# Twelve attention units taken in six pairs: one score run and one softmax for two units

## The chip, the cores and the metric

The kernel runs on one core of a Trainium2 chip. The metric is the device time of one execution in microseconds (us); the time before is the median of three runs, 905.88 us (905.54 to 908.12). One further execution was recorded by the hardware profiler.

## The reference

Attention within chunks of 64 positions, then two dense stages on the 2304 x 512 result, all in float32:

```python
q_c, k_c, v_c = (t.reshape(4, 8, 9, 64, 64) for t in (q, k, v))
s = (q_c @ k_c.transpose(0, 1, 2, 4, 3)) / 8
e = exp(s - s.max(-1)); p = e / (e.sum(-1) + 1e-9)
x = (p @ v_c) as 2304 tokens x 512
x = ((x @ w_a) * (x @ w_b)) @ w_out                      # 512 -> 1536 -> 512
h = x @ w_in                                              # 512 -> 2048
g = (a0 + a1 h + a2 h2 + a3 h3) / (1 + |b0||h| + |b1|h2 + 1e-6)   # h2 = h*h, h3 = h*h*h
out = g @ moe2_w_out                                      # 2048 -> 512
```

## The kernel before

Dense products run as three matmuls each (high by high, high by low, low by high part of the operands, function mm3, whose lines are L252, L253 and L254). They keep TensorE occupied from the first third of the tokens on. The tokens go in three groups of 768. The first group's products with w_a and w_b are plain: 24 entries, each with two products of 128 x 384 outputs (ab_half), and each product is 12 matmuls. The other two groups' products follow in a second part (s_step), which wants the attention output x of these groups in several combinations (x_first, x_second make them on ScalarE and VectorE).

Attention is cut into 18 units of 128 tokens, two chunks of 64 by eight heads. A unit goes through these pieces: T, four PE transposes of k and four of q (a_transpose, L330) and a copy of each out of PSUM on ScalarE (L332); S, 32 score matmuls of 64 x 64 (a_scores, L347), then the maximum and the subtraction on VectorE (L353, L355); X, the exponential on ScalarE (a_exp, L361); E, sum, reciprocal and scaling on VectorE (a_soft, L366 to L369); P, four transposes of the probabilities (a_ptrans, L377) and a copy (L379); V, 32 matmuls of 64 x 64 with v (a_pv, L394) and two copies of the result (L404). Units 0 to 5 make the first token group, units 6 to 11 the second and 12 to 17 the third.

The pieces of the last twelve units are placed between the matmuls of the 24 entries by a list of due times. Every six dense matmuls (half of a product) the function half() first converts a quarter of a weight tile (w_until; L217, L219, L226, L194 on ScalarE, L199, L224, L234 on VectorE), then moves a clock by 0.5 and issues all pieces that are due, in order of due time and then of their entry in the list. Such a half step is called a step here; the times in the list are in units of two steps:

```python
FROM, PER, GAP = 6.0, 2.65, 2.0
times = (0, 0.5, 2, 3, 3.5, 5, 6.5)        # k, q, S, X, E, P, V
a_unit(2 * UH + n, FROM + PER * n + (GAP if n >= 2 * UH else 0), times)
```

PSUM has eight banks: four of pool ps_acc (dense products), one each with the tags a and b (ps_ab, scores and results of V), and two of pool ps_at (transposes), taken in turn. An instruction that writes a bank waits until the reader of what was in it is done. Each engine works through its own instructions in order. The loads of k and q have one buffer each: the load for the next unit is issued (queue SP, in order) behind the transposes that read the present one. Loads of v have two. The loads of raw weight tiles are on the same queue and wait there for the conversion that frees their buffer.

When the third unit of a half group is through V, x_first or x_second puts its passes over x in the list; x_second has fourteen, nine of them on VectorE, due over four time units.

Of the kernel before, what the change touches and what calls it, by code (L numbers as in the profile page):

```python
# [9 lines left out]
F32 = mybir.dt.float32  # L10
# [4 lines left out]
AF = mybir.ActivationFunctionType  # L15
ALU = mybir.AluOpType
AX = mybir.AxisListType
# [3 lines left out]
def chunk_attention_two_mlps(  # L21
# [34 lines left out]
    nc = tc.nc  # L56
    P = 128
    B, H, S, D = q.shape
# [3 lines left out]
    CH = 64  # L62
    NCH = S // CH
    HP = H // 2
    KD = DM // P
# [3 lines left out]
    SCALE = 1.0 / math.sqrt(D)  # L69
# [4 lines left out]
    GH = GT // 2  # L74
    UH = GH // P
    NQ = NT // GT
# [29 lines left out]
    ps_ab = ctx.enter_context(tc.tile_pool(name="ps_ab", bufs=1, space=PSUM))  # L106
    ps_at = ctx.enter_context(tc.tile_pool(name="ps_at", bufs=2, space=PSUM))
# [7 lines left out]
    ident = const.tile([P, P], F32, name="ident")  # L115
# [9 lines left out]
    p_X = s_X.enter_context(tc.tile_pool(name="X", bufs=1))  # L125
    s_x32 = ExitStack()
    p_x32 = s_x32.enter_context(tc.tile_pool(name="x32", bufs=2, side="right"))
# [4 lines left out]
    p_e = const  # L132
# [127 lines left out]
    todo = []  # L260
# [6 lines left out]
    n_todo = [0]  # L267
# [12 lines left out]
    raw = {}  # L280
    un = {}
# [12 lines left out]
    def a_tmp(u, name):  # L294
        if u >= UH:
            return p_t.tile([P, HP, P], F32, name=name, tag="T")
        n = n_t0[0] % 6
        n_t0[0] += 1
        return t_0[n // 3][:, n % 3]

    def a_load(u, *names):

        (b0, c0), (b1, c1) = divmod(2 * u, NCH), divmod(2 * u + 1, NCH)
        for nm, src in (("k", k), ("q", q), ("v", v)):
            if nm not in names or u >= NU:
                continue
            if u < 2 * UH:
                if ("raw", u) not in un:
                    un["raw", u] = p_X.tile([P, 3, H, D], F32, name="kqv", tag=f"X{NQ - 1}_{u + 1}")
                t = un["raw", u][:, "kqv".index(nm)]  # L310
            else:
                t = p_qk.tile([P, H, D], F32, name=nm, tag=nm, bufs=2 if nm == "v" else 1)
            if b0 == b1:
                parts = [(t, src[b0, :, c0 * CH:(c0 + 2) * CH, :])]
            else:
                parts = [
                    (t[c * CH:(c + 1) * CH], src[bb, :, cc * CH:(cc + 1) * CH, :])
                    for c, (bb, cc) in enumerate(((b0, c0), (b1, c1)))
                ]
            for dst, s in parts:  # L320
                nc.sync.dma_start(out=dst, in_=s.rearrange("h s d -> s h d"))
            raw[nm, u] = t

    def a_transpose(u, nm):

        t = raw.pop((nm, u)).rearrange("p (a b) d -> p a (b d)", b=2)
        pool, tag = (ps_acc, "acc") if u < UH else (ps_at, "at")
        ps = pool.tile([P, HP, P], F32, name="at", tag=tag)
        for hp in range(HP):
            nc.tensor.transpose(ps[:, hp, :], t[:, hp, :], ident)  # L330
        o = a_tmp(u, nm + "T")
        nc.scalar.copy(o, ps)  # L332
        un[nm + "T", u] = o

    def a_scores(u):

        qT, kT = un.pop(("qT", u)), un.pop(("kT", u))
        ps = [ps_ab.tile([P, HP, CH], F32, name="at", tag=tag) for tag in "ab"]  # L340
        for a in range(2):
            for c in range(2):
                for t in range(2):
                    for b in range(2):
                        r, half, cols = (slice(n * CH, (n + 1) * CH) for n in (b, t, c))
                        hp = 2 * a + t
                        nc.tensor.matmul(  # L347
                            ps[b][half, 2 * a + c, :], qT[r, hp, cols], kT[r, hp, cols], start=True, stop=True
                        )
        m = p_e.tile([P, 2, HP], F32, name="m", tag="m")  # L350
        e = a_tmp(u, "e").rearrange("p x (y d) -> p (x y) d", d=CH).rearrange("p (b x) d -> p b x d", b=2)
        for b in range(2):
            nc.vector.tensor_reduce(m[:, b], ps[b], AX.X, ALU.max)  # L353
        for b in range(2):
            nc.vector.tensor_tensor(  # L355
                e[:, b], ps[b], m[:, b].unsqueeze(2).to_broadcast([P, HP, CH]), ALU.subtract
            )
        un["e", u] = e.rearrange("p b x d -> p (b x) d")

    def a_exp(u):  # L360
        nc.scalar.activation(un["e", u], un["e", u], AF.Exp, scale=SCALE)  # L361
# [20 lines left out]
    def a_pv(u):  # L382

        pT, vv = un.pop(("pT", u)), raw.pop(("v", u))
        ps = []
        for c in range(2):
            pool, tag = (ps_acc, "acc") if u < UH else (ps_ab, "ab"[c])
            ps.append(pool.tile([P, HP, CH], F32, name="at", tag=tag))
        for hp in range(HP):
            a, t = divmod(hp, 2)  # L390
            for c in range(2):
                for h2 in range(2):
                    r, cols, half = (slice(n * CH, (n + 1) * CH) for n in (c, h2, t))
                    nc.tensor.matmul(  # L394
                        ps[c][cols, hp, :], vv[r, 2 * hp + h2, :], pT[r, 2 * h2 + a, half], start=True, stop=True
                    )
        g, at = divmod(u, 2 * UH)
        if g:
            if at % UH == 0:
                un["x32", g, at // UH] = p_x32.tile([P, KD, GH], F32, name="x32", tag="x32")  # L400
            t = un["x32", g, at // UH]
            for c in range(2):
                to = at % UH * P + c * CH
                nc.scalar.copy(t[:, :, to:to + CH], ps[c])  # L404
            if at % UH == UH - 1:
                (x_first if at < UH else x_second)(g)
            return
        out = [[t[:, :, u * P + c * CH:u * P + (c + 1) * CH] for t in (x_hi, x_lo)] for c in range(2)]
        for c, (hi, lo) in enumerate(out):
            nc.scalar.copy(hi, ps[c])  # L410

        def low():
            for c, (hi, lo) in enumerate(out):
                nc.vector.tensor_tensor(lo, ps[c], hi.bitcast(F32), ALU.subtract)

        un["lo", u] = low

    def x_hl(g, c, x):
        t = x_block(g, c)
        hi, lo = t[:, 0], t[:, 1]  # L420
        return (
            lambda: nc.scalar.copy(hi, x),
            lambda: nc.vector.tensor_tensor(lo, x, hi.bitcast(F32), ALU.subtract),
        )
# [32 lines left out]
    def a_unit(u, at, times):  # L457


        def piece(dt, *fs):  # L460
            for f in fs:
                todo.append((at + dt, n_todo[0], f))
                n_todo[0] += 1

        k, q, s, x, e, p, v = times
        if ("kT", u) not in un:
            piece(k, lambda: a_transpose(u, "k"), lambda: u >= 2 * UH and a_load(u + 1, "k"))
            piece(q, lambda: a_transpose(u, "q"), lambda: u >= 2 * UH and a_load(u + 1, "q"))
        piece(s, lambda: a_scores(u))
        piece(x, lambda: a_exp(u))  # L470
        piece(e, lambda: a_soft(u))
        piece(p, lambda: a_ptrans(u))
        piece(v, lambda: a_pv(u), lambda: u >= 2 * UH and a_load(u + 2, "v"))
        if u < 2 * UH:
            piece(v + 0.5, lambda: un.pop(("lo", u))())


    ca_t = const.tile([P, 4], F32, name="ca_t")
# [219 lines left out]
    y = {}  # L698
# [14 lines left out]
    h2 = {}  # L713
# [111 lines left out]
    for item in FIRST:  # L825
# [9 lines left out]
        what, u = item[:-1], int(item[-1])  # L835
# [12 lines left out]
    seq = [(i, h) for h in range(2) for i in range(4)] + [(i, h) for i in range(4, F1) for h in range(2)]  # L848
    for n in range(UH):
        a_unit(UH + n, 1.0 + 0.5 * n, (0, 0.5, 1.5, 2, 2.5, 3.5, 4.5))  # L850
    FROM, PER, GAP = 6.0, 2.65, 2.0
    times = (0, 0.5, 2, 3, 3.5, 5, 6.5)
    for n in range((NQ - 1) * 2 * UH):
        a_unit(2 * UH + n, FROM + PER * n + (GAP if n >= 2 * UH else 0), times)
    p_j2 = None
    preps = {}

# [12 lines left out]
        if op == 11 and t + 2 < F1:  # L870
            s_load(t + 2)

    END = math.ceil(2 * (FROM + PER * ((NQ - 1) * 2 * UH - 1) + GAP + times[-1] + 0.25)) / 2
    todo.append((END, n_todo[0], s_begin))
    n_todo[0] += 1
    for op in range(12):
        at = min(END + 2 + 0.5 * (op // 3), 2.0 * len(seq) - 0.5)
        todo.append((at, n_todo[0], lambda op=op: s_do(0, op)))
# [29 lines left out]
    for t in range(1, F1):  # L908

        if t == 1:  # L910
            at = [(0, m // 2) for m in range(12)]
        elif t == 2:
            at = [(2, m) for m in (3, 3, 4, 5)] + [(3, m) for m in (0, 1, 2, 3, 3, 4, 5, 6)]
        else:
            at = [(2 * t - 2 + m // 6, FILLS[m % 6]) for m in range(12)]
# [19 lines left out]
    for n, (i, g) in enumerate(seq2):  # L935
        place[:] = [n, 0]
        if n == len(seq2) - 1:
# [3 lines left out]
            t = p_x32.tile([P, 2, SIZES[0]], F32, name="g_raw", tag="x32")  # L941
# [98 lines left out]
```

## Time and profile before

| what | value |
|---|---|
| median of three runs | 905.88 us |
| the profiled execution's own time | 904.24 us |
| its span, first to last instruction | 902.5 us |
| granted TensorE clock over the span | 1.00 |
| busy share of PE, DVE, ACT over the span | 98%, 80%, 68% |
| stretch that holds the last twelve units | about 54 to 172 us |

PE is TensorE, PEld its weight loads, DVE is VectorE, ACT is ScalarE, POOL is GpSimd; SP issues loads. Matmuls overlap one another, so the time that a matmul takes from PE is read from the distance between starts, not from its duration.

### The profile page before, as it was taken

To read this page: it belongs to the slowest core of one execution; us is meant where nothing else is said; L and a number is where in the kernel's file an instruction comes from. 1 tells how busy PE (TensorE), PEld (TensorE's weight loads), DVE (VectorE), ACT (ScalarE), POOL (GpSimd) and SP (SyncE) were. 2 spreads that over 40 slices of the span, in tenths; PEclk is the share of its full clock that TensorE was granted. 3 is DMA by queue.
4 is the path that set the end of the run, shared out by engine and by line. 5 is a ranking of instruction groups with operands and counts; after the bars stand their busy time and mean duration, and the time that the engine had idled before them with its cause. 6 is when DMAs were issued, how large, how long until landed. Compare 5 with 4: busy or idle time off the path is not lost.

```text
span 902.5 us, 14772 instructions
## 1 busy us (share of the span) xinstructions
PE 883.7 (98%) x5532; PEld 788.0 (87%) x5532; DVE 723.3 (80%) x1321; ACT 612.7 (68%) x1105; POOL 63.9 (7%) x122
## 2 busy tenths in 40 slices
PE   6989999999999999999999999999999999999998
PEld 5879989999999999988888998888888888888987
DVE  5657788497878886578778599998889988988886
ACT  5857888445554553678777688877677667776775
POOL 0111111111111111100000000000000000000000
PEclk9999999999999999999999999999999999999999
DMA  9969886333343423778777200200020002000100
GB/s 233 263 200 263 251 239 171 106 130 126 127 146 123 147 85 105 245 250 277 261 243 256 94 1 1 82 1 1 1 93 1 1 1 82 0 1 1 48 1 36
DMA packets 107336, 105.83 MB, mean 117 GB/s; under 512 B 61440, under 2 KB 84480, under 8 KB 107264
## 3 DMA queue, kind: packets, MB, share of 16 engines
q1 hardware_dynamic: 99264, 79.71, 29.6%
q0 software_dynamic: 8000, 25.17, 7.5%
q8 instruction: 43, 0.70, 0.3%
q14 instruction: 29, 0.24, 0.1%
HBM read 74.98 MB, written 29.88 MB: 116 GB/s over the span
## 4 chain that ended last, share of the span: by engine, by line
PE 92%; DVE 4%; ACT 2%; DMA 1%; issue 0%; SPq 0%; DVEq 0%; ACTq 0%
PE h L254 7%; PE acc L254 7%; PE acc L253 7%; PE h L252 7%; PE h L253 7%; PE acc L252 7%; PE acc L682 5%; PE acc L683 5%; PE acc L685 5%; PE ab L252 3%; PE ab L254 3%; PE ab L253 3%; PE y L253 3%; PE y L254 3%; PE y L252 3%; PE q L252 2%
## 5 line engine op out<-in xcount | busy, mean ns | idle before, releaser
L254 PE MATMUL h<-y,w_i 128*128 128x512 f32 (+1 forms) x320 | 117.8, 368 | 0.0
L252 PE MATMUL h<-y,w_i 128*128 128x512 f32 (+1 forms) x320 | 117.8, 368 | 0.0
L253 PE MATMUL h<-y,w_i 128*128 128x512 f32 (+1 forms) x320 | 117.7, 368 | 0.0
L739 ACT ACTIVATE a_ring<-h 128x512 f32<-128x512 f32 (+1 forms) x80 | 44.1, 551 | 88.0 <-PE h L254 88.0
L580 ACT COPY s<-y 128x384 f32<-128x384 f32 x72 | 34.4, 480 | 80.0 <-PE y L254 79.9
L682 PE MATMUL acc<-g_hi,w_o 128*128 128x512 f32 (+1 forms) x240 | 86.9, 369 | 0.0
L683 PE MATMUL acc<-g_hi,w_o 128*128 128x512 f32 (+1 forms) x240 | 86.8, 368 | 0.0
L742 DVE SCALAR_TENSOR_TENSOR u<-u,cb_t,a_ring 128x512 f32<-128x512 f32 (+1 forms) x80 | 55.7, 696 | 30.2 <-ACT u L740 29.4
L254 PE MATMUL acc<-w_o,g_lo 128*128 128x512 f32 x191 | 74.7, 391 | 0.0
L253 PE MATMUL acc<-w_o,g_hi 128*128 128x512 f32 x191 | 74.6, 391 | 0.0
L252 PE MATMUL acc<-w_o,g_hi 128*128 128x512 f32 x191 | 74.3, 389 | 0.0
L253 PEld LDWEIGHTS h<-y,w_i 128*128 128x128 f32 x320 | 60.1, 188 | 8.8
L252 PEld LDWEIGHTS h<-y,w_i 128*128 128x128 f32 x320 | 60.1, 188 | 8.8
L254 PEld LDWEIGHTS h<-y,w_i 128*128 128x128 f32 x320 | 60.1, 188 | 7.4
L662 DVE TENSOR_TENSOR g_lo<-g_raw,g_hi 128x512 fp32r<-128x512 f32 (+1 forms) x60 | 38.2, 638 | 28.1 <-ACT g_hi L660 15.4
L685 PE MATMUL acc<-g_lo,w_o 128*128 128x512 f32 (+1 forms) x240 | 59.3, 368 | 0.0
L741 ACT ACTIVATE t<-h,ca_t 128x512 f32<-128x512 f32 (+1 forms) x80 | 59.0, 737 | 0.0
L752 DVE SCALAR_TENSOR_TENSOR u<-u,r 128x512 f32<-128x512 f32 (+1 forms) x80 | 50.6, 632 | 9.5 <-ACT r L751 9.5
L744 DVE SCALAR_TENSOR_TENSOR t<-t,ca_t,h 128x512 f32<-128x512 f32 (+1 forms) x80 | 55.6, 695 | 2.8
L751 ACT ACTIVATE r<-r,nlsh 128x512 f32<-128x512 f32 (+1 forms) x80 | 54.5, 682 | 2.6
L750 ACT ACTIVATE r<-u,nlsh 128x512 f32<-128x512 f32 (+1 forms) x80 | 55.6, 695 | 0.3
L753 DVE SCALAR_TENSOR_TENSOR t<-t,ca_t,r 128x512 f32<-128x512 f32 (+1 forms) x80 | 55.4, 692 | 0.0
(195 smaller groups left out, 2400.9 us busy)
## 6 DMA issues: line engine op xcount, KB each, us to landing
w_raw<-in_moe_w_out_dram SPq DMA_DIRECT2D x28, 512.0 KB, 3.9
g_d<-g POOLq DMA_DIRECT2D x72, 192.0 KB, 2.5
g_raw<-g_d SPq DMA_DIRECT2D x48, 256.0 KB, 4.2
w_raw<-in_moe_w_in_dram SPq DMA_DIRECT2D x16, 512.0 KB, 4.6
w_raw<-in_moe_w_a_dram SPq DMA_DIRECT2D x12, 512.0 KB, 4.8
w_raw<-in_moe_w_b_dram SPq DMA_DIRECT2D x12, 512.0 KB, 5.2
out_dram<-o SPq DMA_DIRECT2D x18, 256.0 KB, 2.4
y_d<-ys POOLq DMA_DIRECT2D x16, 256.0 KB, 4.1
```

Of the source, the lines that this page charges most:

```text
L252: nc.tensor.matmul(ps, wh, xh, start=first, stop=False, **kw)
L253: nc.tensor.matmul(ps, wh, xl, start=False, stop=False, **kw)
L254: nc.tensor.matmul(ps, wl, xh, start=False, stop=last, **kw)
L682: nc.tensor.matmul(acc[j][d], wh, gh, start=i == 0, stop=False)
L683: nc.tensor.matmul(acc[j][d], wl, gh, start=False, stop=False)
L685: nc.tensor.matmul(acc[j][d], cols(w, d)[0], gl, start=False, stop=i == F1 - 1)
L741: nc.scalar.activation(t, ps, AF.Identity, scale=ca_t[:, 3:4], bias=ca_t[:, 2:3])
L742: nc.vector.scalar_tensor_tensor(u, u, cb_t[:, 0:1], ah, ALU.add, ALU.mult)
L744: nc.vector.scalar_tensor_tensor(t, t, ca_t[:, 1:2], ps, ALU.add, ALU.mult)
L750: nc.scalar.activation(r, u, AF.Ln, scale=2.0 ** -LSH, bias=nlsh[:, 0:1])
L751: nc.scalar.activation(r, r, AF.Exp, scale=-1.0, bias=nlsh[:, 1:2])
L753: nc.vector.scalar_tensor_tensor(t, t, ca_t[:, 0:1], r, ALU.add, ALU.mult)
```

## The change

Units 6 to 17 go in six pairs. A pair has one S of 64 matmuls (a_scores2, a full bank for each of the tags a and b), VectorE's and ScalarE's softmax instructions cover both units (1024 elements per partition where they covered 512, and 512 where 256), and one V of 64 matmuls (a_pv2), whose two result tiles come from ps_at and no longer from ps_ab, each a full bank. T and P stay as four matmuls and a copy for each operand of each unit. Transposed k and q, e and pT of a pair lie in four tiles with one buffer each, in room that was used by the loads of units 2 to 5. The copies out of V are two of 512 elements per pair, or four of 256 where the pair lies in two halves of x. Both loads of v for the next pair are issued behind V. The list of due times becomes:

```diff
-    FROM, PER, GAP = 6.0, 2.65, 2.0
-    times = (0, 0.5, 2, 3, 3.5, 5, 6.5)
-    for n in range((NQ - 1) * 2 * UH):
-        a_unit(2 * UH + n, FROM + PER * n + (GAP if n >= 2 * UH else 0), times)
+    FROM, PER, GAP = 6.0, 5.0, 2.0
+    S_AT, X_AT, E_AT, P_AT, V_AT = 5.0, 6.5, 7.0, 9.0, 10.0
+    def a_pair(u, at):
+        def piece(dt, *fs):
+            for f in fs:
+                todo.append((at + dt, n_todo[0], f))
+                n_todo[0] += 1
+        for x in range(2):
+            for m, nm in enumerate("kq"):
+                piece(x * PER / 2 + m / 2, lambda nm=nm, x=x: a_transpose(u + x, nm), lambda nm=nm, x=x: a_load(u + x + 1, nm))
+        piece(S_AT, lambda: a_scores2(u))
+        piece(X_AT, a_exp2)
+        piece(E_AT, a_soft2)
+        for x in range(2):
+            piece(P_AT + x / 2, lambda x=x: a_ptrans2(u + x))
+        piece(V_AT + 1e-7, lambda: a_pv2(u))
+    for n in range((NQ - 1) * UH):
+        a_pair(2 * UH + 2 * n, FROM + PER * n + (GAP if n >= UH else 0))
...
-    END = math.ceil(2 * (FROM + PER * ((NQ - 1) * 2 * UH - 1) + GAP + times[-1] + 0.25)) / 2
+    END = math.ceil(2 * (FROM + PER * ((NQ - 1) * UH - 1) + GAP + V_AT + 0.25)) / 2
```

```diff
+    def a_scores2(u):
+        qT, kT = un["both", "qT"], un["both", "kT"]
+        ps = [ps_ab.tile([P, 2, HP, CH], F32, name="at", tag=tag) for tag in "ab"]
+        for x in range(2):
+            for a in range(2):
+                for c in range(2):
+                    for t in range(2):
+                        for b in range(2):
+                            r, half, cols = (slice(n * CH, (n + 1) * CH) for n in (b, t, c))
+                            hp = 2 * a + t
+                            nc.tensor.matmul(
+                                ps[b][half, x, 2 * a + c, :], qT[r, x, hp, cols], kT[r, x, hp, cols], start=True, stop=True
+                            )
...
+    def a_pv2(u):
+        pT = un["both", "pT"]
+        ps = [ps_at.tile([P, 2, HP, CH], F32, name="at", tag="at") for c in range(2)]
+        for x in range(2):
+            vv = raw.pop(("v", u + x))
+            for hp in range(HP):
+                a, t = divmod(hp, 2)
+                for c in range(2):
+                    for h2 in range(2):
+                        r, cols, half = (slice(n * CH, (n + 1) * CH) for n in (c, h2, t))
+                        nc.tensor.matmul(
+                            ps[c][cols, x, hp, :], vv[r, 2 * hp + h2, :], pT[r, x, 2 * h2 + a, half], start=True, stop=True
+                        )
...
+        for n in (u + 2, u + 3):
+            a_load(n, "v")
```

With these times the pairs begin at 6, 11, 16, 23, 28 and 33. S falls at 11, 16, 21, 28, 33 and 38, the two P's at 15 and 15.5, 20 and 20.5, 25 and 25.5, 32 and 32.5, 37 and 37.5, 42 and 42.5, and V at 16, 21, 26, 33, 38 and 43. Where pieces share a time, S comes first, then T, then V.

## Rows read from the trace of the kernel before

**Rows 1.** One window: length; PE, PEld, DVE, ACT, POOL busy; clock; DMA share; GB/s.

```profile
54.00:175.00 121.00, 120.25 (x1448) 110.80 (x1441) 85.43 (x180) 87.55 (x170) 18.88 (x35) 1.00 0.71 201
```

**Rows 2.** PE's timeline, first and last of 25 dense matmuls in a row.

```profile
171.72 0.34 PE L253 MATMUL ab<-x_lo,w_a 128*128 128x384 f32 x1
...
175.88 0.33 PE L253 MATMUL ab<-x_lo,w_a 128*128 128x384 f32 x1
```

**Rows 3.** PE's timeline around an S that stands alone.

```profile
76.48 0.34 PE L254 MATMUL ab<-x_hi,w_b 128*128 128x384 f32 x1
76.75 0.69 PE L347 MATMUL at<-kT,qT 64*64 64x64 f32 x32
...
77.65 0.34 PE L253 MATMUL ab<-x_lo,w_b 128*128 128x384 f32 x1
```

**Rows 4.** PE's timeline around four transposes that stand alone.

```profile
86.55 0.34 PE L254 MATMUL ab<-x_hi,w_a 128*128 128x384 f32 x1
86.73 0.60 PE L377 MATMUL at<-ident,e 128*128 128x128 f32 x4
...
87.34 0.34 PE L253 MATMUL ab<-x_lo,w_a 128*128 128x384 f32 x1
```

**Rows 5.** The S of rows 3: its matmuls begun (x) up to two moments.

```profile
76.50:76.86 0.36, 0.12 (x6) 1.00 1.07 258
...
76.50:77.25 0.75, 0.51 (x32) 1.00 1.15 278
```

**Rows 6.** PE's timeline where S stood directly behind another unit's V.

```profile
114.94 0.34 PE L254 MATMUL ab<-x_hi,w_b 128*128 128x384 f32 x1
...
116.37 0.96 PE L347 MATMUL at<-kT,qT 64*64 64x64 f32 x32 [0.46 <-ACT x L404]
...
117.54 0.34 PE L253 MATMUL ab<-x_lo,w_a 128*128 128x384 f32 x1
```

**Rows 7.** PE's timeline where P came before the softmax was ready.

```profile
134.37 0.34 PE L254 MATMUL ab<-x_hi,w_b 128*128 128x384 f32 x1
134.99 0.66 PE L377 MATMUL at<-ident,e 128*128 128x128 f32 x4 [0.28 <-DVE e L369]
...
136.10 0.34 PE L253 MATMUL ab<-x_lo,w_a 128*128 128x384 f32 x1
```

**Rows 8.** PE's timeline around the transposes of a k that were late.

```profile
70.36 0.34 PE L254 MATMUL ab<-x_hi,w_b 128*128 128x384 f32 x1
...
71.32 0.34 PE L253 MATMUL ab<-x_lo,w_b 128*128 128x384 f32 x1
```

**Rows 9.** The chain that ended last: start, time, what; its stretch on DVE.

```profile
117.39 0.74 DVE m L353 x2
...
134.25 0.70 DVE e L369
```

**Rows 10.** PE's timeline, transposes of k and of q of one unit.

```profile
143.69 0.60 PE L330 MATMUL at<-ident,k 128*128 128x128 f32 x4
144.04 0.42 PE L252 MATMUL ab<-x_hi,w_a 128*128 128x384 f32 x1
...
145.17 0.60 PE L330 MATMUL at<-ident,q 128*128 128x128 f32 x4
```

**Rows 11.** ACT's timeline, the copies of these two.

```profile
144.37 0.60 ACT L332 COPY kT<-at 128x512 f32<-128x512 f32 x1
...
146.91 0.57 ACT L332 COPY qT<-at 128x512 f32<-128x512 f32 x1
```

**Rows 12.** Groups by line in 54 to 175: count, busy, mean ns of one.

```profile
L423 DVE TENSOR_TENSOR xs<-x,xs 128x768 fp32r<-128x768 f32 x9 | 8.5, 950 | 0.0
...
L366 DVE TENSOR_REDUCE s<-e 128x8 f32<-128x512 f32 x12 | 8.2, 681 | 0.9 <-ACT e L361 0.8
...
L199 DVE TENSOR_TENSOR w_a<-w_x,w_a 128x512 fp32r<-128x512 f32 x8 | 5.5, 687 | 1.5 <-ACT w_a L194 1.5
```

**Rows 13.** The loads of k: time from issue to landing, all of them.

```profile
DMA to landing us min/median/max: 2.9/4.2/6.1
```

More of the change, by code (lines that the diff above doesn't have):

```diff
@@ L330, in a_transpose @@
             nc.tensor.transpose(ps[:, hp, :], t[:, hp, :], ident)
-        o = a_tmp(u, nm + "T")
+        o = a_tmp(u, nm + "T") if u < 2 * UH else a_both(u, nm + "T")[:, u % 2]
         nc.scalar.copy(o, ps)
@@ L396, in a_pv @@
                     )
[L397 to L407, printed above, removed]
         out = [[t[:, :, u * P + c * CH:u * P + (c + 1) * CH] for t in (x_hi, x_lo)] for c in range(2)]
@@ L416, in a_pv, with a_both @@
         un["lo", u] = low
+    PAIR = {"kT": 3, "qT": 4, "e": 5, "pT": 6}
+    def a_both(u, name):
+        if u % 2 == 0:
+            t = p_X.tile([P, 3, HP, P], F32, name=name, tag=f"X{NQ - 1}_{PAIR[name]}")
+            un["both", name] = t[:, :2]
+        return un["both", name]
+    def a_scores2(u):
[11 more added lines that the diff above has]
+                            )
+        m = p_e.tile([P, 2, 2, HP], F32, name="m2", tag="m2")
+        e = a_both(u, "e").rearrange("p u x (y d) -> p u (x y) d", d=CH).rearrange("p u (b x) d -> p u b x d", b=2)
+        for b in range(2):
+            nc.vector.tensor_reduce(m[:, b], ps[b], AX.X, ALU.max)
+        for b in range(2):
+            nc.vector.tensor_tensor(
+                e[:, :, b], ps[b], m[:, b].unsqueeze(3).to_broadcast([P, 2, HP, CH]), ALU.subtract
+            )
@@ new lines, in a_exp2, with a_soft2 @@
+    def a_exp2():
+        e = un["both", "e"].rearrange("p u x y -> p (u x y)")
+        nc.scalar.activation(e, e, AF.Exp, scale=SCALE)
+    def a_soft2():
+        e = un["both", "e"].rearrange("p u x (y d) -> p (u x y) d", d=CH)
+        s = p_e.tile([P, 2 * H], F32, name="s2", tag="s2")
+        nc.vector.tensor_reduce(s, e, AX.X, ALU.add)
+        nc.vector.tensor_scalar(s, s, 1e-9, None, ALU.add)
+        nc.vector.reciprocal(s, s)
+        nc.vector.tensor_tensor(e, e, s.unsqueeze(2).to_broadcast([P, 2 * H, CH]), ALU.mult)
@@ new lines, in a_ptrans2 @@
+    def a_ptrans2(u):
+        e = un["both", "e"][:, u % 2]
+        ps = ps_at.tile([P, HP, P], F32, name="at", tag="at")
+        for hp in range(HP):
+            nc.tensor.transpose(ps[:, hp, :], e[:, hp, :], ident)
+        nc.scalar.copy(a_both(u, "pT")[:, u % 2], ps)
+    def a_pv2(u):
[3 more added lines that the diff above has]
+            vv = raw.pop(("v", u + x))
+            for hp in range(HP):
+                a, t = divmod(hp, 2)
[4 more added lines that the diff above has]
+                            ps[c][cols, x, hp, :], vv[r, 2 * hp + h2, :], pT[r, x, 2 * h2 + a, half], start=True, stop=True
+                        )
+        for n in (u, u + 1):
+            g, at = divmod(n, 2 * UH)
+            if at % UH == 0:
+                un["x32", g, at // UH] = p_x32.tile([P, KD, GH], F32, name="x32", tag="x32")
+        g, at = divmod(u, 2 * UH)
+        if at % UH < UH - 1:
+            t = un["x32", g, at // UH].rearrange("p k (u c d) -> p u k c d", c=2, d=CH)
+            for c in range(2):
+                nc.scalar.copy(t[:, at % UH:at % UH + 2, :, c], ps[c])
+        else:
+            for x in range(2):
+                t = un["x32", g, (at + x) // UH].rearrange("p k (u c d) -> p u k c d", c=2, d=CH)
+                for c in range(2):
+                    nc.scalar.copy(t[:, (at + x) % UH, :, c], ps[c][:, x])
+        for n in (u, u + 1):
+            at = n % (2 * UH)
+            if at % UH == UH - 1:
+                (x_first if at < UH else x_second)(g)
+        for n in (u + 2, u + 3):
+            a_load(n, "v")
@@ L466, in a_unit @@
         if ("kT", u) not in un:
-            piece(k, lambda: a_transpose(u, "k"), lambda: u >= 2 * UH and a_load(u + 1, "k"))
-            piece(q, lambda: a_transpose(u, "q"), lambda: u >= 2 * UH and a_load(u + 1, "q"))
+            piece(k, lambda: a_transpose(u, "k"))
+            piece(q, lambda: a_transpose(u, "q"))
         piece(s, lambda: a_scores(u))
@@ L472, in a_unit @@
         piece(p, lambda: a_ptrans(u))
-        piece(v, lambda: a_pv(u), lambda: u >= 2 * UH and a_load(u + 2, "v"))
-        if u < 2 * UH:
-            piece(v + 0.5, lambda: un.pop(("lo", u))())
+        piece(v, lambda: a_pv(u))
+        piece(v + 0.5, lambda: un.pop(("lo", u))())
     ca_t = const.tile([P, 4], F32, name="ca_t")
@@ L850, in chunk_attention_two_mlps @@
         a_unit(UH + n, 1.0 + 0.5 * n, (0, 0.5, 1.5, 2, 2.5, 3.5, 4.5))
-    FROM, PER, GAP = 6.0, 2.65, 2.0
-    times = (0, 0.5, 2, 3, 3.5, 5, 6.5)
-    for n in range((NQ - 1) * 2 * UH):
-        a_unit(2 * UH + n, FROM + PER * n + (GAP if n >= 2 * UH else 0), times)
+    FROM, PER, GAP = 6.0, 5.0, 2.0
[11 more added lines that the diff above has]
+        piece(E_AT, a_soft2)
+        for x in range(2):
+            piece(P_AT + x / 2, lambda x=x: a_ptrans2(u + x))
+        piece(V_AT + 1e-7, lambda: a_pv2(u))
+    for n in range((NQ - 1) * UH):
+        a_pair(2 * UH + 2 * n, FROM + PER * n + (GAP if n >= UH else 0))
     p_j2 = None
```

## Prediction

> **What bounds the kernel now.** I read the page's first part, then the window of the twelve units, then PE's timeline in it, then the chain that ended last. PE is busy for 98% of the span (the table above), and in the units' stretch for 120.25 of 121 us at full clock, with VectorE and ScalarE at 71% and 72% and the DMA engines at 0.71 [rows 1]. So a microsecond that a unit's piece takes from PE is a microsecond of the result, and faster VectorE or ScalarE work is worth something only where PE waits for it. Busy says little of how dense PE is, so I count by starts. Dense matmuls start every 173 ns (24 pitches in 4.16 us [rows 2]); six make a step, 1.04 us. Whatever a foreign piece adds is the distance from the dense start before it to the second dense start after it, less two pitches. An S of 32 that stands alone adds 77.65 - 76.48 - 0.35 = 0.82 us [rows 3]; each V alone in the stretch added 0.82 or 0.83 by the same sum, four transposes add 0.44 [rows 4]. Over the stretch that makes 24 x 0.825 + 36 x 0.44 = 35.6 us of pieces. Only three places hold a real wait: S behind another unit's V [rows 6], a P [rows 7], and the transposes of one k [rows 8]. The chain that ended last leaves PE in one place, VectorE work from 117.39 to the P of rows 7 [rows 9]: there x_second's passes and two softmaxes lie back to back.
>
> **What is saved.** The count of small matmuls and transposes stays; what goes is the start and end of blocks. In the S of [rows 3], six matmuls had begun by 76.86 and all 32 by 77.25 [rows 5]: 26 in 0.39 us, 15 ns each (four lie in different quarters of the array at once; with the bins of 30 ns, 14 to 16). A block of 64 therefore adds 0.82 + 32 x 0.0145 = 1.29 us and saves 0.36 against two. Twelve such mergers (six S, six V): 4.3 us, 4.0 to 4.6.
>
> At 21 and 38 V stands directly behind S, both of 64 x 64 form, and one more start and end goes: 0.36 each, 0.7 us. It is 0 at worst: the only such pair before added 2.25 us, and without the 0.46 that S is shown waiting still 1.79, no less than two lone blocks [rows 6]; the wait had parted the two, so I take 0.7. The Trainium skill (TensorEngine Tiling (Array Packing), Key Properties) says that a change of tiling mode drains the engine: by that rule V behind S saves its drain and the sum has the 0.7; by the one pair of the trace it would be 5.6 and not 6.3.
>
> Waits that go: S no longer shares banks with V, so the wait of rows 6 goes: 117.54 - 114.94 - 0.35 - 2 x 0.82 = 0.6 us. The P of rows 7 added 136.10 - 134.37 - 0.35 = 1.38 with the T behind it, 0.5 more than two times 0.44; this goes in its old place (it comes again below). The late k: 71.32 - 70.36 - 0.35 - 0.44 = 0.2 [rows 8]. Sum of what is saved: 4.3 + 0.7 + 1.3 = 6.3 us.
>
> **What is added.** Now V takes both banks of ps_at. At 16 and 33 the order is S, T of k, V; at 26 it is T of q, V. T has just filled one bank, V's first result takes the other, and V's third matmul wants the one that T filled, so PE stands in the middle of its block until ScalarE has copied T out. With an idle ScalarE that copy begins 0.68 us behind the start of T and takes 0.60 [rows 10, 11]; with some 0.05 to PE it is ready 1.33 us behind the start of T. The work behind T starts after 0.35 [rows 10], a V with its change of form at 0.45 or so. The wait is 0.9 us. At 16 and 33 S gives ScalarE 1.2 us to get through its queue first, so I take 0.9 there; at 26 two weight conversions are queued ahead of the copy and I take 1.1. The copy of q in rows 10 and 11 began 1.74 us behind its T, which would make a wait of 1.9. Three places: 2.9 us, from 2.7 to 5.8. At 21, 38 and 43 the banks come from P's, a step and a block earlier, and V needed these copies anyway: nothing, unless the copy begins more than 0.2 us late at 43, where only one step lies between.
>
> The softmax of a pair is longer in latency: two maxima and two subtractions over 512 (0.61 apart, from 681 ns less the overlap; 2.5 us together), an exponential over 1024 (about 1.1, an estimate from copies of 512 that take 0.57 to 0.60 [rows 11]), and sums and scaling over 1024 (a pass of 512 elements costs 681 ns and one of 768 950 [rows 12], so 1.2 each; with the two small ones 2.9). S to P has eight steps, 8.3 us, plus T's and V's between them: 9.5 to 13 us, against 6.5 of its own and 2 to 3 of weights and gates in the queues. Four pairs fit with 1.5 us or more. The fourth (S at 28, P at 32) meets x_second, due from 26.5 on: before its P VectorE has seven passes of x at 0.87 (950 ns less overlap [rows 12]), 6.1; weights and gates, eight at 0.33 to 0.6 (the longest are those of 687 ns [rows 12]), 4.0; its own 2.5 + 2.9. That is 15.4 us, begun about 1.0 behind V (the copies out of it): 16.4. PE gets there in 12 steps, one S and four T's, 12.5 + 1.3 + 1.8 = 15.6. P waits about 0.9 us; the same place cost 0.5 before. Bounds 0 and 2.5. The last pair has no T between S and P; its 9.5 us are just used up, because its exponential comes behind the last weight: 0.2, 0 to 1.
>
> Loads: k and q of the next unit now have five steps and one T, 5.7 us, at the shortest, where the list before left them five or six steps and about two pieces. A load takes 2.9 to 6.1 us, 4.2 in the middle [rows 13], and some 0.5, an estimate, to be issued. Most arrive; those of q issued at 16.5 and 33.5 stand behind two loads of v. I take 0.3, 0 to 1.5. The queue of the weights waits for conversions that I do not see move.
>
> Half as many exponentials and copies save ScalarE a few tenths per pair, hidden under PE. The second part begins when the first ends; s_begin comes half a time unit and the last V a whole one earlier in the list, so nothing there gets later. The shift of buffers to other addresses I cost at nothing, without a row.
>
> Added: 2.9 + 0.9 + 0.2 + 0.3 = 4.3 us. **Net: 6.3 - 4.3 = 2.0 us faster.** In the profiled execution 904.24 would become 902.2 and the span 902.5 become 900.5. That execution lies 1.6 us under the median; against the median, 905.88 - 2.0 = 903.9.
>
> **Rivals.** (a) *V does not wait*: ScalarE or the block order hides the three copies, or P of the fourth pair is in time. Then 4 to 6 us are gained, 900 to 902. For it: S lies between T's predecessor and V, and VectorE's backlog is a sum of overlaps. Against it: rows 10 and 11 put the copy after V's start even with an idle ScalarE. (b) *Grouping saves nothing*: a small matmul costs PE a fixed issue time, and two blocks of 32 cost what one of 64 does. Then 4.3 us of the saving are missing: 908.2. Against it are the starts in [rows 5]. The Trainium skill (TensorEngine Tiling (Array Packing), Instruction Overhead) gives each matmul about 60 cycles, so that an estimate from it, at 2.4 GHz, is 0.8 us for 32; the trace begins 26 in 0.39 us and the rule does not hold for this block. (c) *VectorE becomes the bound, slower*: the pair's softmax is late at every P and not at one. Each of the five others must then be 1.5 to 3 us later than I sum, and from 0.95 us each on (2.0 + 2.7 over five) the kernel is slower by over 0.3%: 908.6 to 911. For it: rows 9 show VectorE without a gap for 17 us already. Against it: 71% busy in the stretch [rows 1], and the fused passes shorten its work. (d) *The copies are all late*, as that of q in rows 11: V waits 5.8 us, and the gain is gone: 906.8.
>
> **How the numbers follow.** About 0.3%, 2.7 us, is what a measurement of this kernel can tell from no change. My forecast, 0.5 to 3.5 us gained (902.4 to 905.4), gets 0.5; a third of its upper part lies beyond 2.7, which is 0.09 of faster. (a) gets 0.27, (b) 0.05, (c) 0.08, (d) 0.1. Faster by over 0.3%: 0.09 + 0.27 = 0.36. Slower by over 0.3%: (c) and a part of (b), 0.10. Within: 0.54. The range from inside (a) to (d), 900.6 to 907, leaves out the best of (a), (b) and (c).
>
> **What would show it.** S and V with 64 matmuls that add 1.3 us to PE each; in V at 16, 26 and 33 a wait of 0.9 to 1.1 us for the copies of k or q; no wait of S for the copies out of V; a P wait near 130 us for VectorE; the first product of the second part begins 2 us earlier. Wrong would make it: a block of 64 that adds over 1.6 us, V waits under 0.3 or over 2 us, P waits at several pairs, or T's that wait for loads.

## The result, and the profile after

The changed kernel is slower: 917.92 us median of four runs (916.41 to 919.31) against 907.0 (905.54 to 908.29) of the kernel before, ratio 1.0121, 95% interval 1.0094 to 1.0148. The forecast was 903.9 us, 900.6 to 907.0. The profiled execution has a span of 914.6 us, 12.1 more than before.

The pieces of the pairs are close to what was forecast. (The program issues 32 small matmuls for a pair's S and 32 for its V, 16 each for one unit; the trace shows each of them as two, so that 64 and 32 are counts of the trace.) PE's timeline of the changed kernel (start, duration, line, operation, count) at 16, where S, T of k and V follow one another, and at 21, where V stands directly behind S:

```profile
82.30 0.34 PE L254 MATMUL ab<-x_hi,w_b 128*128 128x384 f32 x1
82.57 1.16 PE L427 MATMUL at<-kT,qT 64*64 64x64 f32 x64
83.66 0.66 PE L330 MATMUL at<-ident,k 128*128 128x128 f32 x4
84.25 0.33 PE L470 MATMUL at<-pT,v 64*64 64x64 f32 x4
85.05 1.15 PE L470 MATMUL at<-pT,v 64*64 64x64 f32 x60 [0.47 <-ACT kT L332]
86.13 0.44 PE L252 MATMUL ab<-x_hi,w_a 128*128 128x384 f32 x1
86.41 0.34 PE L253 MATMUL ab<-x_lo,w_a 128*128 128x384 f32 x1
...
98.80 0.34 PE L254 MATMUL ab<-x_hi,w_a 128*128 128x384 f32 x1
99.07 1.16 PE L427 MATMUL at<-kT,qT 64*64 64x64 f32 x64
100.05 1.11 PE L470 MATMUL at<-pT,v 64*64 64x64 f32 x64
...
101.38 0.34 PE L253 MATMUL ab<-x_lo,w_b 128*128 128x384 f32 x1
```

The second place adds 101.38 - 98.80 - 0.35 = 2.23 us, against 2 x 0.82 for an S and a V of one unit before [rows 3]. In the first, V begins with four matmuls and then stands until ScalarE has copied k: the place adds 86.41 - 82.30 - 0.35 = 3.76 us. The last V stands alone, and the last P waits:

```profile
163.83 0.34 PE L254 MATMUL ab<-x_hi,w_b 128*128 128x384 f32 x1
164.66 0.63 PE L456 MATMUL at<-ident,e 128*128 128x128 f32 x4 [0.50 <-DVE e L449]
...
165.31 0.34 PE L253 MATMUL ab<-x_lo,w_a 128*128 128x384 f32 x1
...
167.50 0.33 PE L254 MATMUL ab<-x_hi,w_a 128*128 128x384 f32 x1
167.77 1.16 PE L470 MATMUL at<-pT,v 64*64 64x64 f32 x64
...
169.14 0.34 PE L253 MATMUL ab<-x_lo,w_b 128*128 128x384 f32 x1
```

A V of 64 adds 169.14 - 167.50 - 0.35 = 1.29 us. The P adds 165.31 - 163.83 - 0.35 = 1.13, 0.69 over its 0.44 [rows 4].

So where are the 12 us? I cut the execution at PE's first matmul of four kinds: T of unit 6, the first product y of the second part, the first product with w_out, the first h of the last part; the end is the start of the last kind of product. Each difference is worked out from the starts in the trace, in us:

```
                        T6 to y   y to w_out   w_out to h   h to last
before                   125.5      173.9        147.0        397.4
changed                  125.1      177.9        151.2        401.4
```

The units' own part gained 0.4. The other three, in which there are no units, lost 4.0, 4.3 and 4.0 us. Their instructions are the same. Waits explain the smaller share: PE stood idle in them for 1.2, 1.3 and 0.0 us, where before it was 0.0, 0.1 and 0.0. The first two as windows of the changed kernel (length, PE busy, clock, DMA share, GB/s):

```profile
179.53:357.44 177.91, 176.68 (x1004) 1.00 0.35 120
357.44:508.65 151.21, 149.89 (x715) 1.00 0.72 239
```

The rest, over 9 us, is that the dense matmuls have become slower, while the clock is granted in full. PE's timeline of the changed kernel in the second part, first and last of 49 matmuls in a row (48 pitches):

```profile
240.75 0.34 PE L252 MATMUL y<-xs,j_x 128*128 128x384 f32 x1
...
249.19 0.34 PE L252 MATMUL q<-xs,j_x 128*128 128x384 f32 x1
```

That is 8.44 / 48 = 0.1758 us each, where 384 columns took 0.1733 before [rows 2]. And not all of them. By tile (duration min/median/max in ns, first and last start), two groups of the kernel before:

```profile
L253 PE MATMUL q<-xs,j_x x88: 334/334/343, 188.4 to 356.0; 128*128 128x384 f32 x88
L253 PE MATMUL acc<-w_o,g_hi x191: 389/389/397, 512.1 to 895.9; 128*128 128x512 f32 x191
```

The same two and two others in the changed kernel:

```profile
L253 PE MATMUL q<-xs,j_x x88: 336/337/343, 188.0 to 359.6; 128*128 128x384 f32 x88
...
L253 PE MATMUL q<-xs,ws x8: 334/334/342, 181.8 to 208.2; 128*128 128x384 f32 x8
...
L253 PE MATMUL acc<-w_o,g_hi x191: 390/393/404, 520.0 to 907.8; 128*128 128x512 f32 x191
...
L253 PE MATMUL acc<-w_o,g_hl x97: 389/389/397, 524.2 to 909.8; 128*128 128x512 f32 x97
```

The two groups of q do the same work, and so do the two of acc; they differ in where the operands lie. xs, ws, w_o and g_hl are in pools that grow from the left end of SBUF; j_x and g_hi are in pools that grow from the right end. The slow ones are those with one operand from either end; the units' own part has such products too (x_hi from the right end, w_a and w_b from the left), and most of them went from 334 to 337 ns. The change adds two small tiles to the first left pool, m2 of 2 x 2 x 4 and s2 of 16 float32 per partition, 64 bytes each. Every larger left buffer moved by 128 bytes (the first weight tile from byte 17280 to 17408 of a partition), and no right one did (x_hi stays at 171904). By these addresses x_hi lay 154624 bytes, 604 x 256, behind the first weight tile, and in the kernel before the two operands of every dense matmul from the units' part on lie a multiple of 256 bytes apart.

### The profile page after: what moved, and what is told of

The parts are those of the page before. It is cut to its first block, busy times and chain, and to the rows that moved or that the text cites. A ratio compares the mean times of both kernels' runs of the same rounds, so it can differ in the third digit from the quotient of the medians.

```text
span 914.6 us, 14703 instructions
## 1 busy us (share of the span) xinstructions
PE 892.3 (98%) x5532; PEld 793.1 (87%) x5532; DVE 718.7 (79%) x1273; ACT 611.3 (67%) x1091; POOL 64.4 (7%) x122
## 4 chain that ended last, share of the span: by engine, by line
PE 81%; DVE 1%; ACT 1%; DMA 1%; issue 0%; SPq 0%; DVEq 0%; ACTq 0%
PE acc L254 7%; PE acc L253 7%; PE h L254 7%; PE h L252 7%; PE acc L252 7%; PE h L253 7%; PE acc L757 5%; PE acc L760 5%; PE acc L758 5%; PE y L254 3%; PE y L252 3%; PE y L253 3%; PE q L252 2%; PE q L254 2%; PE q L253 2%; PE ab L252 1%
## 5 line engine op out<-in xcount | busy, mean ns | idle before, releaser
L655 ACT COPY s<-y 128x384 f32<-128x384 f32 x72 | 34.4, 479 | 84.3 <-PE y L254 84.0
L757 PE MATMUL acc<-g_hi,w_o 128*128 128x512 f32 (+1 forms) x240 | 87.9, 373 | 1.2 <-ACT g_hi L735 1.2
L758 PE MATMUL acc<-g_hi,w_o 128*128 128x512 f32 (+1 forms) x240 | 87.7, 372 | 0.0
L252 PE MATMUL acc<-w_o,g_hi 128*128 128x512 f32 x191 | 75.5, 395 | 0.0
L253 PE MATMUL acc<-w_o,g_hi 128*128 128x512 f32 x191 | 75.4, 395 | 0.0
L735 ACT CAST g_hi<-g_raw 128x512 fp32r<-128x512 f32 (+1 forms) x60 | 34.5, 576 | 31.3 <-PE acc L758 24.9
```

The source lines that it names most:

```text
L252: nc.tensor.matmul(ps, wh, xh, start=first, stop=False, **kw)
L253: nc.tensor.matmul(ps, wh, xl, start=False, stop=False, **kw)
L757: nc.tensor.matmul(acc[j][d], wh, gh, start=i == 0, stop=False)
L758: nc.tensor.matmul(acc[j][d], wl, gh, start=False, stop=False)
```

## The experiments

Theory A: this shift makes the matmuls slower, and the pairs are innocent. Theory B: the pairs or the order of work do it, through waits or the clock. "Old addresses" below means that the old m and s share the tags of m2 and s2 and that the filler in the pool shrinks from 24 to 8 floats:

```diff
-        m = p_e.tile([P, 2, HP], F32, name="m", tag="m")
+        m = p_e.tile([P, 2, 2, HP], F32, name="m", tag="m2")[:, :, 0]
-        s = p_e.tile([P, H], F32, name="s", tag="s")
+        s = p_e.tile([P, 2 * H], F32, name="s", tag="s2")[:, :H]
-    const.tile([P, 24], F32, name="pad_l", tag="pad_l")
+    const.tile([P, 8], F32, name="pad_l", tag="pad_l")
```

**The pairs with the old addresses** (e1).

> The pairs as changed, but the two new small tiles of the softmax take the place of the old ones and the filler in that pool is smaller, so that every larger buffer lies where it lay before. Theory A (the 128 bytes by which the left buffers moved against the right ones make the dense matmuls slower): the pitch of the 384-column matmuls is 0.1733 us again and not 0.1759, the span about 900.9 us, 1.6 under that of before, ratio 0.998. Theory B (the pairs and their order of work do it, by waits or by the clock): pitch 0.176 and about 915 to 918 us, as the changed kernel.

Measured: 907.37 us against 906.11, ratio 1.0005 (0.9993 to 1.0016). The loss is gone, and the forecast gain isn't there either, of which below.

**The kernel before, with the left buffers 128 bytes further** (e2): `pad_l` of 56 floats, nothing else.

> The kernel before with 128 bytes more of filler in the left pool, nothing else. Theory A: the loss of the changed kernel without its gain, pitch 0.176, 10 to 14 us slower than before, ratio 1.011 to 1.015. Theory B: no change, ratio 1.000.

Measured: 915.38 us, ratio 1.0097 (1.0082 to 1.0113). The kernel before, without a single pair, loses most of what the changed kernel lost, and the pairs without the shift lose nothing (e1). Theory B falls as the reason for the loss.

**The changed kernel with the right buffers moved too** (e3): `pad_r` of 56 floats.

> The changed kernel with the right buffers moved by 128 bytes too. If it is the place of one operand against the other that matters (A, relative): as with the old addresses, 905 us, ratio 0.998. If it is the address itself, 0 or 128 beyond a multiple of 256 (A, absolute): all dense matmuls slow, over 918 us. Theory B: 915 to 918 us.

Measured: 907.52 us, ratio 1.0009 (0.9997 to 1.0020). The addresses are all 128 bytes off the old ones and it is as fast as with the old ones: the place of left and right buffers against each other matters, not the address.

**The kernel before, left buffers 256 bytes further** (e4): `pad_l` of 88 floats.

> The kernel before with 256 bytes more of filler in the left pool. Theory A with a period of 256 bytes: ratio 1.000. A with a longer period, or distance as such: slower by 5 to 14 us. Theory B: ratio 1.000.

Measured: 905.53 us, ratio 0.9995 (0.9982 to 1.0009). Nothing is lost, so it is not the distance as such. The group of q in its trace:

```profile
L253 PE MATMUL q<-xs,j_x x88: 334/334/337, 190.3 to 357.9; 128*128 128x384 f32 x88
```

**The kernel before, left buffers 64 bytes further** (e5): `pad_l` of 40 floats.

> The kernel before with 64 bytes more of filler in the left pool. The distance of left and right operands is then 64 beyond a multiple of 256. If what hurts is half of the period alone, ratio 1.000; if any distance that is no multiple of 256 does, 1.005 to 1.010 with the pitch of the 384-column matmuls at 0.175 to 0.176 us in the second part.

Measured: 909.79 us, ratio 1.0045 (1.0030 to 1.0059). Half the loss, but not spread as expected: the second part took 174.0 us, as before; the products with w_out took 151.0 and lost 4.0 us, of which 1.2 us are a wait of PE for ScalarE's copy g_hi. The same groups in the traces of e1, e2, e3 and e5, in this order, one fence each:

```profile
L253 PE MATMUL q<-xs,j_x x88: 334/334/339, 190.6 to 359.8; 128*128 128x384 f32 x88
```

```profile
L253 PE MATMUL q<-xs,j_x x88: 336/337/343, 190.3 to 360.2; 128*128 128x384 f32 x88
```

```profile
L253 PE MATMUL q<-xs,j_x x88: 334/334/338, 187.6 to 356.7; 128*128 128x384 f32 x88
```

```profile
L682 PE MATMUL acc<-g_hi,w_o x240: 276/393/393, 354.7 to 509.1; 128*128 128x512 f32 x96, 128*128 128x256 f32 x24
L683 PE MATMUL acc<-g_hi,w_o x240: 276/398/398, 354.8 to 509.4; 128*128 128x512 f32 x96, 128*128 128x256 f32 x24
...
L253 PE MATMUL acc<-w_o,g_hl x97: 389/389/397, 521.2 to 903.4; 128*128 128x512 f32 x97
```

337 where left and right were moved against each other by 128, 334 where they were not; at 64 the product with operands from both ends takes 393 to 398 where the one from the left end alone takes 389. With 64 bytes no product of 384 columns lost time, neither in the second part (moving operand from the left end) nor in the units' part (from the right end, 125.5 us as before); most of those of 512 with operands from both ends did.

That leaves the gain of about 2 us that e1 and e3 did not show. In the parts of the execution (one profiled execution each; the third part also holds waits of PE of 0.1 to 1.5 us that come and go without the shift):

```
                        T6 to y   y to w_out   w_out to h   h to last
before                   125.5      173.9        147.0        397.4
e4 before, 256           125.9      173.9        148.2        397.4
e5 before, 64            125.5      174.0        151.0        398.0
e2 before, 128           126.4      176.3        150.1        401.4
e1 pairs, old addresses  124.8      175.5        148.7        397.4
e3 pairs, both moved     123.9      175.5        147.2        397.4
e8 x_second later        126.4      173.9        147.2        397.4
e9 T later, last later   123.3      173.9        147.4        397.4
e7 V alone               122.0      173.9        147.9        397.5
e11 V alone, timed       121.8      173.9        148.1        397.4
e10 V alone, gap 2.5     122.2      175.7        146.9        397.4
```

e3 gained 1.6 us in the units' part, and e1 0.6, where two T's cost 0.9 us more than alone. Both then lost 1.6 us in the second part, where the pairs are over. The traces of the changed kernel and of e1 show the place; the changed kernel on PE and on DVE, then DVE before:

```profile
188.05 0.34 PE L253 MATMUL q<-xs,j_x 128*128 128x384 f32 x1
188.99 0.44 PE L254 MATMUL q<-xs,j_x 128*128 128x384 f32 x1 [0.61 <-DVE j_x L627]
```

```profile
186.18 0.95 DVE L499 TENSOR_TENSOR xs<-x,xs 128x768 fp32r<-128x768 f32 x1
187.04 0.42 DVE L632 TENSOR_TENSOR wf<-wf 128x256 f32<-128x256 f32 x1
187.38 0.95 DVE L499 TENSOR_TENSOR xs<-x,xs 128x768 fp32r<-128x768 f32 x1
188.25 1.29 DVE L627 TENSOR_TENSOR j_x<-wf,j_x 128x512 fp32r<-128x512 f32 x2
```

```profile
187.08 1.29 DVE L552 TENSOR_TENSOR j_x<-wf,j_x 128x512 fp32r<-128x512 f32 x2
188.29 1.82 DVE L423 TENSOR_TENSOR xs<-x,xs 128x768 fp32r<-128x768 f32 x2
```

The last V comes one time unit earlier in the list, x_second is due a fixed 5.5 behind it, and so two more passes over x (L499, L423 before) now lie in front of the second part's weights (L627, L552 before), for which PE waits 0.61 us; 8 us later it waits 0.62 us for a copy of ScalarE (s, L655).

**x_second as late as before** (e8): the old addresses, and

```diff
-        at = 0.5 if g < NQ - 1 else 5.5
+        at = 0.5 if g < NQ - 1 else 6.5
```

> As the pairs with the old addresses, but the last group's x_second is due 6.5 time units behind the last V and not 5.5, as late against the matmuls as before the change. If the 1.5 us that the part from the first product y to the first product with w_out lost (175.5 against 173.9 us) come from these passes falling into the preparation of the second part's weights, that part takes 173.9 us again, and the time is 1 to 2 us under that of before, ratio 0.998. If they come from something else (the order of the last V, buffers), 175.5 us and ratio 1.0005 stay.

Measured: the second part took 173.9 us again and both waits are gone, so the reason holds. The time was 906.3 against 905.93 us, ratio 1.0001 (0.9991 to 1.0010): no gain. In its profiled execution (906.78 us) one T of k waited 1.8 us for its load and the units' part took 126.4 us; whether that held in the others wasn't seen.

**No T in front of a V** (e9): the old addresses, and

```diff
-    FROM, PER, GAP = 6.0, 5.0, 2.0
-    S_AT, X_AT, E_AT, P_AT, V_AT = 5.0, 6.5, 7.0, 9.0, 10.0
+    FROM, PER, GAP = 6.0, 5.0, 2.5
+    T_AT, S_AT, X_AT, E_AT, P_AT, V_AT = 0.5, 5.0, 6.5, 7.0, 9.0, 10.0
...
-                piece(x * PER / 2 + m / 2, lambda nm=nm, x=x: a_transpose(u + x, nm), lambda nm=nm, x=x: a_load(u + x + 1, nm))
+                piece(T_AT + x * PER / 2 + m / 2, lambda nm=nm, x=x: a_transpose(u + x, nm), lambda nm=nm, x=x: a_load(u + x + 1, nm))
+        d = 0.5 if u == NU - 2 else 0
...
-            piece(P_AT + x / 2, lambda x=x: a_ptrans2(u + x))
-        piece(V_AT + 1e-7, lambda: a_pv2(u))
+            piece(P_AT + d + x / 2, lambda x=x: a_ptrans2(u + x))
+        piece(V_AT + d + 1e-7, lambda: a_pv2(u))
...
-    END = math.ceil(2 * (FROM + PER * ((NQ - 1) * UH - 1) + GAP + V_AT + 0.25)) / 2
+    END = math.ceil(2 * (FROM + PER * ((NQ - 1) * UH - 1) + GAP + V_AT + 0.75)) / 2
```

> Old addresses; all T's half a time unit later and the gap 2.5, so that no T stands directly before V, and the last pair's P and V half a unit later, which puts x_second back to its old place too. If V's waits are for the bank that T filled: the three waits of together 2.9 us go, V adds 0.92 behind S and 1.29 alone, the last P waits less than 0.4, and with the second part at 173.9 us the time is 4 to 5 us under that of before, ratio 0.995. If V's waits have another cause (the copies of pT, ScalarE's queue), they stay and the ratio is 0.998 to 1.000.

Measured: 902.97 against 905.93 us, ratio 0.9973 (0.9958 to 0.9988). No V waits: four times S and V add 2.22 or 2.23, two V's alone 1.29 or 1.30, and the last P does not wait. The second part took 173.9 us. It is less than hoped; in the profiled execution two T's of q waited 2.6 and 1.3 us for their loads, the longer one here:

```profile
98.38 1.08 PE L330 MATMUL at<-ident,q 128*128 128x128 f32 x4 [2.59 <-DMA q<-in_q_dram]
```

**Every V one time unit later** (e7, one execution): the old addresses and `V_AT = 11.0`.

> Old addresses; every V one time unit later, so that it stands between dense matmuls, with no T and no S next to it. If T's bank is what V waits for, each of the six V's adds 1.29 us and no more; against the pairs with the old addresses the first part gains 2.9 of waits and loses 0.7 of the two V's that stood behind S.

Measured: 902.78 us in one run, the units' part 122.0 us, six V's of 1.29 or 1.30. The place that added 3.76 in the changed kernel is now, in the trace of e11, the same kernel:

```profile
83.63 1.16 PE L427 MATMUL at<-kT,qT 64*64 64x64 f32 x64
84.72 0.66 PE L330 MATMUL at<-ident,k 128*128 128x128 f32 x4
...
87.85 1.16 PE L470 MATMUL at<-pT,v 64*64 64x64 f32 x64
88.94 0.45 PE L252 MATMUL ab<-x_hi,w_b 128*128 128x384 f32 x1
```

S with T adds 1.68 there and V 1.30, 2.98 in all; V's wait at 16 was 0.8 us.

**The same, timed** (e11).

> The kernel with every V one time unit later, timed. Its first part took 122.0 us in one look against 125.5 before, and its second part 173.9 as before. If these parts are what the time is made of, 3 to 3.5 us under that of before, ratio 0.996 to 0.997; if the start of the kernel or late loads take it back, 0.998 to 1.000.

Measured: 904.16 against 905.98 us, ratio 0.9971 (0.9959 to 0.9984). With the old addresses and this order, pairs beat the kernel before by 0.3%.

**And with a gap of 2.5** (e10): `GAP = 2.5`.

> As that one, with the gap before the last three pairs 2.5 and not 2.0. The P at 132.9 us waited 0.96 us for VectorE, which had x_second in front of it; with a step more between, it adds 0.44 and the time is 0.5 to 1 us less, ratio 0.995 to 0.996. If the second part's weights come late because everything behind moves, that part takes over 174 us and the ratio is 0.997 to 0.999.

Measured: 904.96 us, ratio 0.9988 (0.9973 to 1.0002). The P behind x_second still cost 0.8 us more than alone, and the second part took 175.7 us: PE waited 0.73 us there for a result of VectorE (b, L697). x_second moved with V, which may be why; that was not tried apart. No gain; the second half of the expectation is what happened.

The times of one kernel spread over up to 6 us, before as after. One source is seen in e1's windows (length, PE busy, clock, DMA share, GB/s): near the start the granted clock fell to 0.50, the lower level of 1.2 GHz, behind waits of PE of 1.1 to 2.3 us. The profiled execution of before had 1.00 there, although PE was idle for as long in its first 54 us, 14.0 us against 12.7; why the clock fell in one and not in the other stays open.

```profile
0.00:30.00 30.00, 20.56 (x269) 0.77 0.93 238
19.90:23.00 3.10, 2.00 (x36) 0.50 0.93 239
```

## Why the prediction was wrong

The step that failed is one sentence: "The shift of buffers to other addresses I cost at nothing, without a row." It had neither a bound nor a rival, and it was worth 9 to 11 us: 8.8 in the kernel before (e2), and 10.5 between the changed kernel (1.0121) and the same with the old addresses (1.0005). The price is 1.4% on products that occupy PE nearly all of the time, 0.1758 against 0.1733 us. By part it was about 1.2 us among the units (125.1 against e3's 123.9), 2.4 in the second part (177.9 against 175.5), 3.0 in the products with w_out (less the waits) and 4.0 behind them. It alone put the time outside the range, and none of the four rivals had it.

A second step failed: "s_begin comes half a time unit and the last V a whole one earlier in the list, so nothing there gets later." Earlier work on VectorE stood in front of the second part's weights: 1.6 us (e1 and e3 against e8).

The other steps, against the trace of the changed kernel and e3:

- Mergers: 1.29 us for a block of 64, as worked out. The rival that grouping saves nothing is refuted.
- V behind S: 2.23 against 2 x 1.29, 0.35 saved each, as taken; the one pair of rows 6, which a wait had parted, was no guide. The Trainium skill (TensorEngine Tiling (Array Packing), Key Properties) says that a change of tiling mode drains the engine. The trace agrees so far that two blocks of one form, directly behind each other, save 0.35 us.
- V's waits for T's bank: the places at 16, 33 and 26 added 3.76, 3.98 and 2.64 us. Without the wait the first two are 2.97 (1.68 for S and T, 1.29 for V, e7) and the third 1.73 (0.44 and 1.29): 0.8, 1.0 and 0.9 us, 2.7 in all against 2.9 forecast. e9 and e7 take T away from V and the wait goes, so the cause is shown. Rival (a) is refuted as far as V goes. The places at 26 and 33 in the changed kernel:

```profile
115.70 1.15 PE L470 MATMUL at<-pT,v 64*64 64x64 f32 x60 [0.58 <-ACT qT L332]
139.40 1.15 PE L470 MATMUL at<-pT,v 64*64 64x64 f32 x60 [0.69 <-ACT kT L332]
```

- P of the fourth pair: 0.44 us too much in the changed kernel, 0.9 in e3, 0.9 forecast. (The forecast's terms on VectorE add up to 15.5 us and not 15.4; that changes nothing.)
- P of the last pair: 0.69 and 0.8 against 0.2. Mis-sized. In the changed kernel a pass over x (L499, 158.03) stood in front of the weight conversions and the exponential began at 160.34; in e11, with V later, the exponential began at 158.02, the passes came behind it and this P adds 0.44 and waits for nothing, as in e7 and e10. What makes it was not tried alone.
- T's that came too early, for loads above all: 0.9 us in the changed kernel, none in e3, 2.0 at one place in e8, against 0.3. It varies from execution to execution.

Without the shift, the units' part gained 1.6 us in e3 where 2.0 were forecast, and the second part took 1.6 of it back.

## What to carry to other kernels

A new tile of 64 bytes is not free because it is small: it moves everything behind it in its pool. Compare the pitch of the same dense matmuls, far from the change, before looking for waits; if it changed at full clock, put the buffers back where they were before judging the change. And work that is moved earlier on an engine that is not the bound can push back what the bound needs next.

## What the hardware showed that was not expected

A dense matmul whose moving and stationary operands lie in buffers from both ends of SBUF took 334 ns (384 columns) or 389 (512) when they were a multiple of 256 bytes apart, as in the kernel before, e3 and e4. With 128 bytes off (the changed kernel, e2) it took 337 and 392 to 395, with a pitch of 0.176 against 0.173 us for 384 columns. With 64 bytes off (e5) it took 336 in the second part, at the old pitch, and 393 to 398 in the products with w_out. Products with both operands from the left end did not change when they stood among their like (ws, g_hl). The products h, which also have both operands from there, did in part:

```profile
L252 PE MATMUL h<-y,w_i x320: 333/389/389, 500.8 to 889.7; 128*128 128x512 f32 x96, 128*128 128x384 f32 x64
L252 PE MATMUL h<-y,w_i x320: 333/389/398, 508.7 to 901.5; 128*128 128x512 f32 x96, 128*128 128x384 f32 x64
```

The first line is of the kernel before, the second of the changed one. Of the twelve matmuls of an h of 512 columns there, the first took 397 ns on the mean where a product with g_hi stood in front, the tenth 389 again, and the last 396 where one stood behind; next to products with g_hl it was 389 throughout. So a slow product also slows some of the matmuls next to it.

Three shifts were tried (64, 128 and 256), so a period of 256 bytes fits them, but what in the chip makes it stays open. Why 64 bytes spare the products of 384 columns and cost those with w_out, of 512, about 2.9 us, as much as 128 bytes do, and the last part, also of 512, only 0.6 us, is open too.
